# Attention output normalized in feature layout with its product on GpSimd; tanh in place of GELU for the middle chunks; gated-unit weights in 15 parts

## The chip, the core and the metric

The kernel runs on one core of one Trainium2 chip. A core has five engines that run side by side, each with a queue of its own: TensorE (PE; its weight loads are listed as PEld), VectorE (DVE), ScalarE (ACT), GpSimd (POOL) and SyncE (SP), which here only issues transfers (DMA). They wait for one another with semaphores. The metric is device microseconds for one execution, the median of several runs.

## The reference

One transformer block in bfloat16: layer norm, attention with 32 heads of 20 features over 2048 tokens, layer norm, and a gated unit of width 1728 with a GELU in its tanh form.

```python
B, S, D, H, Dh, Df = 1, 2048, 640, 32, 20, 1728

def _A_ref(x, wqkv, wo):
    q, k, v = split of (x @ wqkv) into [3][B, H, S, Dh]
    scores = einsum("bhqd,bhkd->bhqk", q, k) * Dh ** -0.5
    o = einsum("bhqk,bhkd->bhqd", softmax(scores), v)
    return o.reshape(B, S, D) @ wo

def _B_ref(x, w_gate, w_up, w_down):
    return (gelu(x @ w_gate, approximate=True) * (x @ w_up)) @ w_down

h = x + _A_ref(_layernorm(x), wqkv, wo)
return h + _B_ref(_layernorm(h), w_gate, w_up, w_down)
```

## The kernel before, in words

**A planner writes the order.** The kernel does not issue instructions as it goes. Each operation is recorded by `op(...)` with an engine, an estimated duration, a priority, what it reads and writes and which banks of the accumulator memory (PSUM, eight banks of 512 columns) it takes and returns. `Sched.schedule` then plays the program through with these estimates and fixes an order for each engine's queue; `Sched.emit` writes it out with the semaphore waits it needs. Each queue is in order: an instruction that waits holds up all behind it. Where TensorE would be idle too long, the planner puts in filler matmuls (`sc.warm`, which reads `kt_all`). A switch of ScalarE's function table is charged by `MODE_SWITCH`. Nearly all operations recorded through the small helper `I` carry the line of that helper in the profile (L357), so groups are told apart by their tiles.

**Stages.** First come the loads of x, the layer norm and the projections of keys, queries and values (L632). Keys and queries are written to DRAM and read back into `kt_all` and `qt_all` in rows of four heads, 32 partitions each (`k_rows`, `q_rows`; `bounds` is a row that keeps the exponentials in range).

**Attention.** The tokens are cut into seven query chunks, `SIZES = (512, 512, 256, 256, 256, 128, 128)`, called chunks 0 to 6. A chunk is worked off in slots; a slot covers four heads times 512 columns, so there are 8 + 8 + 3 x 4 + 2 x 2 = 32 slots. In a slot TensorE computes scores (L911) into two alternating groups of banks, ScalarE takes their exponentials in bites of 1024 and 1536 columns (`pts`, and `pts2` which lies in `rege`), and TensorE multiplies with the values (L357, `v_all`). For about a ninth of the score tiles VectorE forms the exponential instead: an eviction (L832), then four integer scalings of 128x2048 (`d_exp`). One column of the values is 1, so row 20 of each block of 32 partitions sums the exponentials.

**Epilogue of a slot** (`epilogue`). VectorE copies the output from PSUM to `osb`, with features on partitions and tokens on columns. TensorE transposes it in fp32 (L976), VectorE takes the reciprocal of the sums (L982) and multiplies (L985) into `o_nat`, tokens on partitions.

**After a chunk** (`post`). `o_nat` is transposed back to features (`oT`): for chunk 0 and the last one by TensorE (L577), for the others by a transposing DMA. Then comes the product with `wo`, the residual, the layer norm (its root by a chain of small GpSimd operations, for the last chunk by ScalarE), a transpose to `hnT`, and the gated unit: gate matmuls (L1053) evicted by VectorE (L1088), GELU on ScalarE in place over up to 2048 columns, up matmuls (L1053 again) and their product (L1099), down matmuls (L1110), the sum (L1114) and the store. All this runs as background of the next chunk's attention, at low priority. The last chunk (`tail`) has nothing to run behind; there GELU reads PSUM directly (L1075).

**The gated unit's weights** lie in `regw`, where the projections' data lay before, so they are loaded once all readers of these are through: three big loads and a rest.

```python
load(wg, B_w_gate.rearrange("(a p) f -> p a f", p=128), "wg", 11.0, after=wr)
load(wu, B_w_up.rearrange("(a p) f -> p a f", p=128), "wu", 16.0, after=wr)
load(wd[:, 0:NF - 1, :], B_w_down[0:(NF - 1) * 128, :].rearrange("(a p) d -> p a d", p=128),
     "wd", 21.0, after=wr)
```

Of the kernel before, what the change touches and what calls it, by code (L numbers as in the profile page):

```python
# [7 lines left out]
ALU = mybir.AluOpType  # L8
# [35 lines left out]
class Sched:  # L44
# [46 lines left out]
    def schedule(self):  # L91
# [23 lines left out]
        while done < total:  # L115
# [4 lines left out]
            for e in ENGINES:  # L120
# [208 lines left out]
D_FIRST, D_SPAN = 0, 18  # L329
RSQRT_MAGIC = float(0x5F3759DF)  # L330
# [5 lines left out]
def bass_sequential_preLN__mha_block__glu_gated_geglu__prompt_kernel(  # L336
# [12 lines left out]
    with ExitStack() as es:  # L349
# [10 lines left out]
        def c_mm(n, passes=1):  # L360
            return 0.004 + passes * n / 2400.0
# [31 lines left out]
        o_nat = sb("o_nat", [128, 4, D])  # L393
# [566 lines left out]

        def epilogue(s_, bk):
            s = s_ % 2
            c, gs = slots[s_]
            nq = CHUNKS[c][1]
            nt = nq // 128
            op("dve", I("tensor_copy", osb[:, s, :], PS[:, 512 * 6:512 * 7]), c_dve(512), P_QK,
               reads=[("O", s_)], writes=[("osb", s)], rel=[bk])
            b2 = Bank(*BG[c])
            key = ("bk", sc_id())
            aft = set()  # L970
            tb = base(c)
# [27 lines left out]

        def post(c, banks, tail):  # L1000
# [5 lines left out]
            first = tuple(e_ops) + tuple(last_qk[0]) + tuple(d_ops) if c == 0 else ()  # L1006
            for tt in range(tb, tb + nt):
                t = q0 // 128 + tt - tb
                i = t % 2
                if tail or c == 0:  # L1010
                    transposes(o_nat[:, tt, :], [("on", g, tt) for g in range(NG)], oT[:, :, tt * 128:(tt + 1) * 128],
                               ("hnT", tt), banks, P_EPI, "act" if tail else "dve", after=first)
                else:
                    dma_transposes(o_nat[:, tt, :], [("on", g, tt) for g in range(NG)], oT[:, :, tt * 128:(tt + 1) * 128],
                                   ("hnT", tt), after=first)
# [31 lines left out]
            def mms(k, w, wkey, after):  # L1047
                bk, key = Bank(*banks), ("bk", sc_id())
                for fi in range(min(fn_, NF - k * fn_)):
                    f = k * fn_ + fi  # L1050
                    for a in range(NA):
# [4 lines left out]
                           c_mm(nq), p, mode="full", util=nq / 2400.0, reads=hk + [wkey], writes=[key], acq=[bk] if st else [],  # L1056
# [45 lines left out]
            for tt in range(tb, tb + nt):  # L1102
                t = q0 // 128 + tt - tb
                i = t % 2
                for hf in range(2):
                    bk = Bank(*banks)
                    key = ("bk", sc_id())
                    for f in range(NF):
# [3 lines left out]
                            start=(f == 0), stop=(f == NF - 1)), c_mm(320), p, mode="full", util=0.133, reads=hkeys(f // fn_) + ["wd", "wdz"],  # L1112
# [23 lines left out]
        for s_, (c, gs) in enumerate(slots):  # L1136
            if c == 0:
# [17 lines left out]
                if g == 7:  # L1155
                    wr = tuple(w_readers)
                    load(wg, B_w_gate.rearrange("(a p) f -> p a f", p=128), "wg", 11.0, after=wr)
                    load(wu, B_w_up.rearrange("(a p) f -> p a f", p=128), "wu", 16.0, after=wr)
                    load(wd[:, 0:NF - 1, :], B_w_down[0:(NF - 1) * 128, :].rearrange("(a p) d -> p a d", p=128),
                         "wd", 21.0, after=wr)  # L1160
                    r0 = (NF - 1) * 128 - F0[-1]
                    load(wd[r0:128, NF - 1, :], B_w_down[(NF - 1) * 128:DFF, :], "wd", 2.6, after=wr)
# [40 lines left out]
```

## Time and profile before

| | before |
|---|---|
| median of 3 runs (912.53 to 921.97) | 912.77 us |
| profiled execution, its own time | 915.09 us |
| span in its profile, first to last instruction | 913.2 us |
| TensorE busy | 861.3 us (94%) |
| ScalarE busy | 859.8 us (94%) |
| VectorE busy | 651.7 us (71%) |
| GpSimd busy | 33.2 us (4%) |
| mean granted TensorE clock | 0.993 |
| exponentials on ScalarE (`pts` and `rege` from `ps`) | 825.2 us in 693 instructions |
| function table loads on ScalarE | 16, of 1.28 us each |
| fp32 transposes on TensorE (L976) | 128, 26.8 us |

The groups of a profile are given as: line, engine, operation, out<-in tiles with partitions x elements, count, busy time, mean duration. Busy time of an engine is the union of its instructions' times; TensorE's counts a matmul from start to a modelled end. A row of the timeline has start, duration, engine, line, form and, in brackets, how long the engine was idle before and who ended that.

### The profile page before, as it was taken

To read this page: it belongs to the slowest core of one execution; us is meant where nothing else is said; L and a number is where in the kernel's file an instruction comes from. 1 tells how busy PE (TensorE), PEld (TensorE's weight loads), DVE (VectorE), ACT (ScalarE), POOL (GpSimd) and SP (SyncE) were. 2 spreads that over 40 slices of the span, in tenths; PEclk is the share of its full clock that TensorE was granted. 3 is DMA by queue.
4 is the path that set the end of the run, shared out by engine and by line. 5 is a ranking of instruction groups with operands and counts; after the bars stand their busy time and mean duration, and the time that the engine had idled before them with its cause. 6 is when DMAs were issued, how large, how long until landed. Compare 5 with 4: busy or idle time off the path is not lost.

```text
span 913.2 us, 24238 instructions
## 1 busy us (share of the span) xinstructions
PE 861.3 (94%) x10905; PEld 371.0 (41%) x10905; DVE 651.7 (71%) x1210; ACT 859.8 (94%) x775; POOL 33.2 (4%) x117
## 2 busy tenths in 40 slices
PE   3999999999999999999999998999999999999998
PEld 2532222222232222222344443333444456666677
DVE  7838797888888968877777785665556766654453
ACT  6699999989999989999999999999999999999960
POOL 5000000000001000000000010000001100010100
PEclk9999999999999989999999999999999999999999
DMA  7211020230100380000100101000101001000100
GB/s 259 86 46 32 13 56 6 61 89 22 50 8 12 64 295 1 1 1 1 31 9 17 38 2 31 1 1 2 38 23 45 17 2 24 25 17 10 39 9 23
DMA packets 39519, 34.43 MB, mean 38 GB/s; under 512 B 19436, under 2 KB 36936, under 8 KB 39416
## 3 DMA queue, kind: packets, MB, share of 16 engines
q1 hardware_dynamic: 39416, 32.89, 12.8%
q8 instruction: 85, 1.39, 0.6%
q14 instruction: 18, 0.15, 0.1%
HBM read 20.12 MB, written 8.09 MB: 31 GB/s over the span
## 4 chain that ended last, share of the span: by engine, by line
PE 46%; ACT 45%; DVE 5%; DMA 2%; issue 0%; SPq 0%; DVEq 0%
ACT pts L357 34%; PE ps L911 13%; PE ps L357 11%; ACT rege L357 10%; PE ps L1053 7%; PE ps L632 7%; PE ps L1110 6%; DMA regw<-in_A_wqkv_dram 1%; DVE rege L832 1%; DVE rege L357 1%; DMA rege<-in_A_x_dram 1%; DVE qt_all L832 1%; ACT L357 1%; PE ps L976 1%; DVE qt_all L357 1%; PE ps L577 0%
## 5 line engine op out<-in xcount | busy, mean ns | idle before, releaser
L357 ACT ACTIVATE pts<-ps 128x1536 bf16<-128x1536 f32 x578 | 652.0, 1252 | 14.8 <-PE ps L911 8.8
L911 PE MATMUL ps<-qt_all,kt_all 32*128 32x256 bf16 (+2 forms) x3584 | 322.4, 290 | 20.2 <-ACT pts L357 11.2
L911 PEld LDWEIGHTS ps<-qt_all,kt_all 32*128 32x128 bf16 x3584 | 102.9, 92 | 236.9 <-ACT pts L357 130.2
L832 DVE TENSOR_SCALAR rege<-ps 128x512 int16<-128x512 f32 x200 | 137.4, 688 | 73.3 <-PE ps L911 71.2
L357 ACT ACTIVATE rege<-ps 128x1536 bf16<-128x1536 f32 x115 | 173.2, 1506 | 1.6 <-PE ps L911 1.1
L1053 PE MATMUL ps<-rege,regw 128*128 128x256 bf16 (+2 forms) x980 | 154.5, 290 | 3.8 <-DVE rege L1099 2.3
L357 PE MATMUL ps<-pts,v_all 128*21 128x256 bf16 (+2 forms) x2472 | 135.0, 288 | 0.0
L357 PE MATMUL ps<-rege,v_all 128*21 128x512 bf16 (+2 forms) x1564 | 127.9, 316 | 1.4 <-DVE rege L357 1.0
L832 DVE TENSOR_SCALAR qt_all<-ps 128x512 int16<-128x512 f32 x116 | 79.8, 688 | 49.1 <-PE ps L911 48.4
L1053 PEld LDWEIGHTS ps<-rege,regw 128*128 128x128 bf16 x980 | 74.3, 98 | 57.8 <-issue 26.1
L357 DVE TENSOR_SCALAR rege<-rege 128x2048 int16<-128x2048 int16 x132 | 88.8, 685 | 2.4 <-PE ps L357 1.1
L632 PE MATMUL ps<-regw 128*128 128x512 bf16 (+1 forms) x360 | 87.5, 352 | 2.0 <-DVE rege L832 0.9
L1110 PE MATMUL ps<-regw,rege 128*128 128x320 bf16 x448 | 80.1, 301 | 1.1 <-DVE rege L832 0.5
L357 PEld LDWEIGHTS ps<-pts,v_all 128*21 128x21 bf16 x2472 | 54.3, 91 | 34.6 <-issue 28.3
L357 PEld LDWEIGHTS ps<-rege,v_all 128*21 128x21 bf16 x1564 | 41.3, 91 | 44.0 <-issue 24.4
L357 PE MATMUL ps<-qt_all,v_all 128*21 128x256 bf16 (+2 forms) x1048 | 53.7, 284 | 2.1 <-DVE qt_all L357 2.0
L1099 DVE TENSOR_TENSOR rege<-rege,ps 128x512 bf16<-128x512 bf16 (+1 forms) x53 | 36.0, 680 | 27.2 <-PE ps L1053 27.2
L1110 PEld LDWEIGHTS ps<-regw,rege 128*128 128x128 bf16 x448 | 37.1, 98 | 29.9 <-issue 13.8
L632 PEld LDWEIGHTS ps<-regw 128*128 128x128 bf16 x360 | 29.2, 99 | 47.6 <-issue 26.3
L1088 DVE CAST rege<-ps 128x512 bf16<-128x512 f32 (+1 forms) x53 | 36.1, 680 | 16.2 <-PE ps L1053 16.0
L357 DVE TENSOR_SCALAR qt_all<-rege 128x2048 int16<-128x2048 int16 x70 | 47.0, 686 | 0.7
L357 DVE TENSOR_SCALAR qt_all<-qt_all 128x2048 int16<-128x2048 int16 x69 | 46.3, 685 | 1.7 <-PE ps L357 1.3
(92 smaller groups left out, 483.7 us busy)
## 6 DMA issues: line engine op xcount, KB each, us to landing
rege<-in_A_x_dram SPq DMA_DIRECT2D x6, 640.0 KB, 5.2
q_rows<-regw SPq DMA_DIRECT2D x20, 128.0 KB, 1.7
out_dram<-rege SPq DMA_DIRECT2D x16, 160.0 KB, 1.9
regw<-in_B_w_gate_dram SPq DMA_DIRECT2D x1, 2160.0 KB, 10.6
regw<-in_B_w_up_dram SPq DMA_DIRECT2D x1, 2160.0 KB, 15.6
regw<-in_B_w_down_dram SPq DMA_DIRECT2D x1, 2080.0 KB, 21.6
kt_all<-k_rows SPq DMA_DIRECT2D x12, 160.0 KB
qt_all<-q_rows SPq DMA_DIRECT2D x12, 160.0 KB
```

The lines of the kernel that those rows point to most:

```text
L357: return lambda eng: getattr(eng, method)(*args, **kwargs)
L632: yield op("pe", lambda eng, l=l, r=r, k=k: eng.matmul(bank(bk, n), l, r, start=(k == 0), stop=(k == len(steps) - 1)), c_mm(n), prio, mode ...
L832: d_ops.append(op("dve", lambda eng: eng.tensor_scalar(v[:, 512 * h:512 * h + 512], bank(b), EXP_MUL, -32000.0, ALU.mult, ALU.max), c_dve( ...
L911: return lambda eng: eng.matmul(out()[:, kk * nq:(kk + 1) * nq], kt_all[32 * j:32 * j + 32, g, kt * 128:(kt + 1) * 128], qt_all[32 * j:32 ...
L976: op("pe", lambda eng, tt=tt: eng.transpose(bank(b2)[:, tt * 128:(tt + 1) * 128], osb[:, s, tt * 128:(tt + 1) * 128], identf[:]), c_mm(128 ...
L1053: op("pe", lambda eng, a=a, f=f, fi=fi: eng.matmul(bank(bk)[:, fi * nq:(fi + 1) * nq], w[:, a, F0[f]:F0[f] + 128], hnT[:, a, 128 * tb:128 ...
L1088: cp.append(op("dve", lambda eng, bg=bg, fv=fv, w=w: eng.tensor_copy(fv, bank(bg, w)), c_dve(w), p, reads=[kg], writes=hkeys(k), rel=[bg], ...
L1099: hdone.append(op("dve", lambda eng, bu=bu, fv=fv, w=w: eng.tensor_tensor(fv, fv, bank(bu, w), ALU.mult), c_dve(w), p, reads=[ku] + hkeys( ...
L1110: op("pe", lambda eng, f=f, o=o, hf=hf, bk=bk: eng.matmul(bank(bk, 320), ha_f[:, o:o + 128], wd[:, f, hf * 320:(hf + 1) * 320], start=(f = ...
```

## The change

**Output.** For all chunks but the last, `epilogue` ends after the copy to `osb` and calls the new function `spread`. The four rows of sums go to DRAM and come back as 128 x 16 numbers; VectorE takes their reciprocals there; these go to DRAM and come back as `bsum`, each row repeated over the 32 partitions of its head. GpSimd multiplies `osb` with `bsum` into `on16`, which four transfers store by head into a DRAM tensor of the chunk. `post` then loads `oT` from it in one transfer. `o_nat` remains for the last chunk alone.

**GELU.** For chunks 1 to 5 the eviction of the gate halves it, and the new function `gelu` works on two tiles at a time: with v half the gate, VectorE forms v(a + b v v), ScalarE takes its tanh, VectorE adds 1 and multiplies with v. The buffer `zb` becomes two of 1024, read as float16. The operation's mode is `exp2`, for which the planner charges no table switch. Chunk 0 and the last chunk keep their GELU.

**Weights.** Gate and up weights are loaded in five parts each, the down weights in five, besides the rest; each part waits for the one before the last, and matmuls wait for both of the two semaphores.

```diff
-                if o.mode is not None:
+                if o.mode is not None and o.mode != "exp2":
...
+GELU_A = 2.0 * 0.7978845608028654
+GELU_B = 4.0 * GELU_A * 0.044715
...
-        o_nat = sb("o_nat", [128, 4, D])
+        bsum = sb("bsum", [128, 512], FP32)
+        on16 = sb("on16", [128, 512])
+        o_nat = sb("o_nat", [128, 1, D])
...
-        zb = carve(2 * 512).rearrange("p (i s) -> p i s", i=2)
+        zb = carve(2 * 1024).rearrange("p (i s) -> p i s", i=2)
+        tb16 = zb.bitcast(F16)
...
+        sdr = nc.dram_tensor("sums", [2, 4, 512], FP32, kind="Internal").ap()
+        rdr = nc.dram_tensor("rsums", [2, 4, 512], FP32, kind="Internal").ap()
+        adr = [nc.dram_tensor("attn%d" % c, [NG, 4, DH, n], BF16, kind="Internal").ap() for c, (_, n) in enumerate(CHUNKS[:-1])]
...
+        def spread(s, c, gs, nq):
+            n = len(gs)
+            h = lambda dst, src, reads, key, sem, issue: dma(dst, src, key, reads, sem + str(s), 3.2, P_EPI, issue, keep=False)
+            h(sdr[s], osb[DH:128:32, s, :], [("osb", s)], ("sdr", s), "sa", 0.1)
+            h(rc[:, s, :], sdr[s].rearrange("j (a b) -> (j a) b", b=16), [("sdr", s)], ("rc", s), "sb", 0.4)
+            op("dve", I("reciprocal", rc[:, s, :], rc[:, s, :]), 0.25, P_EPI, reads=[("rc", s)], writes=[("rc", s)])
+            h(rdr[s].rearrange("j (a b) -> (j a) b", b=16), rc[:, s, :], [("rc", s)], ("rdr", s), "sc", 0.4)
+            for j in range(4):
+                h(bsum[32 * j:32 * j + 32, :], rdr[s, j].partition_broadcast(32), [("rdr", s)], ("bs", j), "sd", 0.36)
+            op(POOL, I("tensor_tensor", on16[:], osb[:, s, :], bsum[:], ALU.mult), 1.4, P_EPI,
+               reads=[("osb", s)] + [("bs", j) for j in range(4)], writes=["on16"])
+            for j in range(4):
+                h(adr[c][gs[0]:gs[0] + n, j].rearrange("g e s -> e g s"),
+                  on16[32 * j:32 * j + DH, :].rearrange("p (g s) -> p g s", g=n), ["on16"], ("adr", c, gs[0], j), "se", 0.36)
...
+            if c < len(CHUNKS) - 1:
+                spread(s, c, gs, nq)
+                return
...
+        def gelu(k, w, fv, hk, p):
+            i = gelu_n[0] % 2
+            gelu_n[0] += 1
+            z, zk = tb16[:, i, 0:w], ("zb", i)
+            tt, ts = 0.066 + w * 0.0006, 0.156 + w * 0.00026
+            op("dve", I("tensor_tensor", z, fv, fv, ALU.mult), tt, p, reads=hk, writes=[zk], after=tuple(last_qk[1]))
+            op("dve", I("tensor_scalar", z, z, GELU_B, GELU_A, ALU.mult, ALU.add), ts, p, reads=[zk], writes=[zk])
+            op("dve", I("tensor_tensor", z, z, fv, ALU.mult), tt, p, reads=hk + [zk], writes=[zk])
+            op("act", I("activation", z, z, ACT.Tanh), c_act(w) + 0.04, -1, mode="exp2", reads=[zk], writes=[zk])
+            op("dve", I("tensor_scalar", z, z, 1.0, None, ALU.add), ts, p, reads=[zk], writes=[zk])
+            op("dve", I("tensor_tensor", fv, z, fv, ALU.mult), tt, p, reads=hk + [zk], writes=hk)
...
+            if not tail:
+                op("sp", I("dma_start", oT[:, :, 128 * tb:128 * tb + nq],
+                           adr[c].rearrange("g j e s -> (g j e) s").rearrange("(a p) s -> p a s", p=128)), 0.4, P_EPI,
+                   reads=[("adr", c, gs[0], j) for cc, gs in slots if cc == c for j in range(4)],
+                   writes=[("hnT", tt) for tt in range(tb, tb + nt)], sem=f"oT{c}", lat=2.4 + nq * 0.001, after=first)
...
-                if tail or c == 0:
-                    transposes(o_nat[:, tt, :], ...)
-                else:
-                    dma_transposes(o_nat[:, tt, :], ...)
+                if tail:
+                    transposes(o_nat[:, 0, :], ...)
...
+                    if c:
+                        op("dve", lambda eng, bg=bg, fv=fv, w=w: eng.tensor_scalar(fv, bank(bg, w), 0.5, None, ALU.mult),
+                           c_dve(w), p, reads=[kg], writes=hkeys(k), rel=[bg])
+                        if k % 2 or k == nb - 1:
+                            gelu(k - k % 2, w + 512 * (k % 2), hv(k - k % 2, w + 512 * (k % 2)),
+                                 hkeys(k - 1) * (k % 2) + hkeys(k), p)
+                        continue
...
-                for ks in [list(range(i, min(i + 4, nb))) for i in range(0, nb, 4)]:
+                for ks in [] if c else [list(range(i, min(i + 4, nb))) for i in range(0, nb, 4)]:
...
+                    parts = [(wg[:, a, :], B_w_gate[128 * a:128 * a + 128, :], "wg") for a in range(NA)]
+                    parts += [(wu[:, a, :], B_w_up[128 * a:128 * a + 128, :], "wu") for a in range(NA)]
+                    parts += [(wd[:, f:min(f + 3, NF - 1), :], B_w_down[128 * f:128 * min(f + 3, NF - 1), :].rearrange(
+                        "(a p) d -> p a d", p=128), "wd") for f in range(0, NF - 1, 3)]
+                    ids = []
+                    for i, (dst, src, key) in enumerate(parts):
+                        ids.append(op("sp", I("dma_start", dst, src), 0.35, P_EPI, sem="wp%d" % (i % 2), lat=3.4,
+                                      writes=[(key, i % 2)], after=tuple(wr) if i < 2 else ids[-2:-1]))
```

More of the change, by code (lines that the diff above doesn't have):

```diff
@@ L970, in epilogue @@
             aft = set()
-            tb = base(c)
+            tb = 0
             for g in gs:
@@ L998, in prefetch @@
                after=tuple(e_ops) + tuple(w_readers) if c == 0 else ())
+        gelu_n = [0]
+        def gelu(k, w, fv, hk, p):
[9 more added lines that the diff above has]
+            op("dve", I("tensor_tensor", fv, z, fv, ALU.mult), tt, p, reads=hk + [zk], writes=hk)
         def post(c, banks, tail):
@@ L1009, in post @@
                 i = t % 2
-                if tail or c == 0:
-                    transposes(o_nat[:, tt, :], [("on", g, tt) for g in range(NG)], oT[:, :, tt * 128:(tt + 1) * 128],
-                               ("hnT", tt), banks, P_EPI, "act" if tail else "dve", after=first)
-                else:
-                    dma_transposes(o_nat[:, tt, :], [("on", g, tt) for g in range(NG)], oT[:, :, tt * 128:(tt + 1) * 128],
-                                   ("hnT", tt), after=first)
+                if tail:
+                    transposes(o_nat[:, 0, :], [("on", g, 0) for g in range(NG)], oT[:, :, tt * 128:(tt + 1) * 128],
+                               ("hnT", tt), banks, P_EPI, "act", after=first)
                 for hf in range(2):
@@ L1055, in mms @@
                             start=(a == 0), stop=(a == NA - 1)),
-                           c_mm(nq), p, mode="full", util=nq / 2400.0, reads=hk + [wkey], writes=[key], acq=[bk] if st else [],
+                           c_mm(nq), p, mode="full", util=nq / 2400.0, reads=hk + [(wkey, 0), (wkey, 1)], writes=[key], acq=[bk] if st else [],
                            after=after if st else ())
@@ L1111, in post @@
                             bank(bk, 320), ha_f[:, o:o + 128], wd[:, f, hf * 320:(hf + 1) * 320],
-                            start=(f == 0), stop=(f == NF - 1)), c_mm(320), p, mode="full", util=0.133, reads=hkeys(f // fn_) + ["wd", "wdz"],
+                            start=(f == 0), stop=(f == NF - 1)), c_mm(320), p, mode="full", util=0.133, reads=hkeys(f // fn_) + [("wd", 0), ("wd", 1), "wd2", "wdz"],
                            writes=[key], acq=[bk] if f == 0 else [], after=hdone[-2:] if f == 0 else ())
```

6 lines of the change are left out of this document (1 added, 5 removed).

## The prediction

> **What bounds the kernel now.** I read the busy times first, then busy time by stage, then the ScalarE timeline, then what lies behind the last exponential. These are the page's totals, and busy time in five windows (columns: from and to, length, then busy us and instruction count of PE, PEld, DVE, ACT, POOL; granted clock; DMA share; GB/s).
>
> ```profile
> PE 861.3 (94%) x10905; PEld 371.0 (41%) x10905; DVE 651.7 (71%) x1210; ACT 859.8 (94%) x775; POOL 33.2 (4%) x117
> ```
>
> ```profile
> 47.00:265.00 218.00, 206.80 (x1722) 61.54 (x1719) 174.65 (x310) 211.80 (x188) 0.00 (x0) 0.99 0.14 39
> 265.00:480.00 215.00, 206.06 (x1935) 64.94 (x1934) 171.30 (x294) 211.94 (x185) 3.31 (x15) 0.98 0.16 44
> 480.00:740.00 260.00, 250.46 (x3643) 112.03 (x3641) 177.99 (x321) 259.36 (x226) 10.58 (x42) 1.00 0.08 19
> 740.00:873.20 133.20, 129.57 (x2969) 85.96 (x2967) 72.77 (x136) 132.83 (x115) 7.17 (x28) 1.00 0.08 20
> 873.20:913.20 40.00, 36.16 (x420) 29.41 (x417) 17.26 (x39) 11.07 (x15) 0.00 (x0) 1.00 0.05 18
> ```
>
> From 47 to 873.2 us ScalarE is idle for 10.3 of 826 us (6.2, 3.1, 0.6 and 0.4), so each microsecond that leaves ScalarE there moves the last exponential forward. TensorE looks as full, but what it does besides scores and values fills gaps: from 480 us on ScalarE is idle for 1.0 of 393 us, whatever it waits for. VectorE has 20% to 45% left by stage. Behind the last exponential (873.24) come 40.0 us in which ScalarE works 11 and TensorE 36. So the time is ScalarE's stream plus a tail.
>
> This is what stands between the exponentials of chunk 4 (ScalarE timeline: start, us, form):
>
> ```profile
> 866.33 1.28 ACT L357 ACT_TABLE_LOAD   x1
> 867.62 3.28 ACT L357 ACTIVATE rege<-rege 128x2048 bf16<-128x2048 bf16 x2
> 870.92 1.28 ACT L357 ACT_TABLE_LOAD   x1
> 872.22 1.02 ACT L357 ACTIVATE pts<-ps 128x1024 bf16<-128x1024 f32 x1
> ```
>
> Two table loads enclose the GELU of each chunk: 5.89 us from 866.33 to 872.22. Chunks 2 and 3 cost the same, chunk 1 (7168 columns) 9.07 us.
>
> **GELU as tanh.** Removed from ScalarE's full stretch: 9.07 + 3 x 5.89 = 26.7 us (chunk 0 keeps its GELU). Added: the built order shows 16 tanhs of 1024 columns and 3 of 512 before the last exponential, and no table load beside them (6 loads in all, 16 before). An exponential of 1024 follows the one before by 0.92 us, a pass over 1024 columns in SBUF lasts 1.04 alone; I take 0.95. For 512, 0.60 alone less the 0.1 of overlap: 0.5. 16 x 0.95 + 3 x 0.5 = 16.7. **Gain 10.0 us**, between 8.3 (all at 1.04, and 0.6) and 10.6 (0.92, 0.48).
>
> VectorE pays. Each pair of gate tiles gets three products and two scalings over 1024 columns. Rows: a bf16 product of 1024 takes 690 ns, of 512 413; a scaling of 2048 takes 685, of 512 286, hence about 419 for 1024. So 2.91 us for each of 17 pairs, 1.81 for each of three single tiles, 2.4 for the last 768: 57 us. Leaving VectorE: 30 of 32 reciprocals (254 ns, 7.6), the products at L985 of all but chunk 6 (17.2) and four copies at L586 (1.9); a reciprocal in SBUF comes back 30 times, at 0.17 to 0.25 (6). Net +36: 688 us, 75% of the span. If the mixed float16 and bfloat16 products ran at the pace of an fp32 eviction (512 in 0.68, so about 1.2 for 1024), 27 us more, 78%. Between 250 and 320 us VectorE is 90% busy while ScalarE idles 0.1 us, so I cost both at nothing. The cover is VectorE's idle time; without it a tanh waits for its input, with all exponentials queued behind it. The halving at the gate's eviction replaces a copy of the same size (688 against 685 ns): nothing. **Bounds 0 and +5** (19 tanhs, each 0.26 late).
>
> **Normalization.** TensorE loses 120 fp32 transposes of 128 columns (26.8 us for 128 of them: 25.1) and 20 bf16 ones (2.2). TensorE ended almost no ScalarE wait after chunk 1, so in the stream this is worth nothing; it moves background work forward. The built order has the following behind the last score matmul: 260 matmuls of 128 columns instead of 274, none of 256 instead of 70, 86 of 320 instead of 112. At 57, 115 and 142 ns (127 in 7.25 us, 27 in 3.12, 28 in 3.98) that is 0.8 + 8.1 + 3.7 = 12.6 us less.
>
> Of this the tail gets little. From 873.24 to the feature transposes at 888.17, the chain of chunk 6 (values, copy, reciprocal, output product, statistics, square root) waits for TensorE for 1.4 + 0.7 + 0.7 and for a late chunk-5 GELU with two table loads, 1.9 (884.1 to 886.0): 4.7 saved. But VectorE now runs chunk 5's scaling chain between these steps (two products of 0.6, one of 0.5, two scalings of 0.3, a longer eviction: 2.7 less 0.8 that lay there before), and the second tanh holds ScalarE's copy of the transposes by about 0.8: 2.7 back. What follows the transposes is 210 matmuls of 128 and 56 of 320 in both. **Tail -2.0 us**, between +2 and -5.
>
> SyncE gets 11 small transfers for each of 30 slots, 330 at 0.31 to 0.55 us of issue, some 116 us of an idle queue, and loses 11 transposing ones (1.2 each). The chain is: sums out, sums in, reciprocal, back out, four broadcasts, product, four stores, and one load per chunk. Six landings in a row at 1.6 (bounds) to 2.7 us (transposes), 3 of issue, 1.5 of arithmetic: 14 to 21 us where transposes and copies took about 4. It is covered by the next chunk's slots of 25 us (two for the last such chunk). Without the cover chunk 5 comes up to 17 us later into the tail, which then pays perhaps 5. Small transfers also queue behind big ones:
>
> ```profile
> 186.70 0.41 SPq L357 DMA_DIRECT2D rege<-in_A_x_dram  x1
> 187.16 0.55 SPq L357 DMA_DIRECT2D qt_all<-bounds  x1
> ...
> 192.12 1.02 ACT L357 ACTIVATE pts<-ps 128x1024 bf16<-128x1024 f32 x1 [3.40 <-PE ps L911]
> ```
>
> The bounds go behind 640 KB, and ScalarE waits 3.40 us. The order keeps this pair, so this stays. The new reciprocal waits in VectorE's queue for such a transfer: what is late behind it are the evictions of scores, then value matmuls.
>
> **Weights in 15 parts.** 6.4 MB, two parts of some 430 KB in flight instead of all at once; the three loads landed 22 us after issue. At the 400 GB/s of that stretch the data alone take 16, with 2 us of landing behind each pair 31; I take 24, and 0 for the time: the gate's first matmul comes about two slots after the first part. At worst +2.
>
> **GpSimd's product.** No product of this size is in the trace. Below: a memset of 128x512 fp32, 0.54 us. Above: a one-input select over 160 columns is 0.35, 0.95 ns a column beyond 0.2, so two inputs over 512 give 1.2; with one VectorE operation waited for, 1.9. It is nearest to the select; I take 1.2. What it does to VectorE is the larger matter:
>
> ```profile
> 546.05 0.20 POOL L357 TENSOR_TENSOR rs<-rs,nw 128x4 f32<-128x4 f32 x1
> 546.33 0.70 POOL L357 TENSOR_TENSOR nw<-rs 128x4 f32<-128x4 f32 x1
> ...
> 546.27 0.69 DVE L357 TENSOR_SCALAR qt_all<-rege 128x2048 int16<-128x2048 int16 x1
> ```
>
> The same small product takes 0.20 alone and 0.70 when a 2048-column scaling started 0.06 earlier: it ends 0.07 behind that. So the two exclude each other, and a product of 1.2 us that starts first should hold the next such scaling for up to 1.2. Thirty of these cost VectorE up to 36 us. What reaches ScalarE is less: TensorE waits for about 90 of 318 such scalings already (27 us in all), and scores have room, since their weight loads wait for ScalarE 360 times, 0.36 us each. One product in three, 0.35 us each: **+3.5 us**, bounds 0 and 30 x 1.0.
>
> The Trainium skill's "SBUF — State Buffer", section "Who interferes with whom", says that GpSimd and such a VectorE operation hold a shared pair of ports for the whole instruction and the second one fully blocks. The rows agree for GpSimd as the second; no run here shows VectorE as the second. By this rule the 3.5 us stand; if VectorE were not held as the second, the sum below would be -12.0 and the time 900.8.
>
> **Sum.** -10.0 - 2.0 + 3.5 = -8.5. The profiled execution's span of 913.2 becomes 904.7, its own time 915.09 becomes 906.6. That execution lies 2.3 above the median of the runs (912.77); on the median: **904.3 us**. 1% is 9.1 us, about what a measurement of this kernel can tell from no change.
>
> **Rivals.** *Lock:* GpSimd's product holds VectorE at a scaling that value matmuls wait for, every slot; TensorE's queue is in order, so scores come late too. For it: the rows above, and 27 us of such waits now. Against it: idle VectorE time and 130 us in which TensorE waits for ScalarE. It eats 12.0 us from 0.40 us a slot on; at 0.8 the time is 912.8 + 12 = 925.
>
> *Clock:* with the transposes gone TensorE has less to do while the weights arrive. From 318 to 334 us the granted clock was 0.70 and ScalarE lost 2.6 of 16 us. The built order ends the projections two slots earlier and starts the gate at the same slot: up to 50 us thin, with 27 filler matmuls there instead of 7. At half of it, 25 x 2.6/16 = 4, at all of it 8: the gain is gone, about 911.
>
> *Clean:* no new stall, and half of the ScalarE idle time of the first two stages (9.3) leaves with the transposes: -10 - 2 - 4.6, 896.
>
> That the change doesn't do what it says is out for the tables: the built order has 6 loads.
>
> **How the numbers follow.** Forecast 0.58 (900 to 909 by its own bounds, a little under half of it under 903.6); clean 0.15; clock 0.13; lock 0.14, nearly all over 922. Faster by over 1%: 0.27 + 0.15 = 0.42; slower by over 1%: 0.13; within: 0.45. The range leaves out the upper part of the lock and the lower end of clean: 895 to 919.
>
> **What would show it.** Right: 6 table loads; last exponential at 864 to 869 us; tanhs with no idle time before them; 37 to 40 us behind the last exponential; TensorE busy near 835. The lock: GpSimd's products over 1.2 us, VectorE's 2048-column scalings over 0.69, ScalarE idle in stages beyond 480 us. The clock: granted clock under 0.9 over more than 16 us. I am wrong if VectorE passes 80%, or if ScalarE waits for tanh inputs.

## The result, and the profile after

The changed kernel takes 919.41 us (median of 20 executions, 914.35 to 924.12) against 913.02 (20 executions, 911.88 to 921.97): ratio 1.0053, interval 1.0031 to 1.0074, so 3 to 7 us slower. The forecast was 904.3, the range ended at 919.0. The profiled execution is one of the shortest: 914.51 us, span 912.7. The twenty differ by TensorE's mean granted clock: seven with 0.983 to 0.985 take 914.35 to 917.40, thirteen with 0.970 to 0.978 take 918.19 to 924.12.

The page's totals after the change:

```profile
PE 851.5 (93%) x10792; PEld 358.4 (39%) x10792; DVE 688.1 (75%) x1263; ACT 849.0 (93%) x775; POOL 75.2 (8%) x147
```

VectorE is where the prediction put it (688). ScalarE lost 10.8 us. TensorE lost only 9.8, though 120 fp32 and 20 bf16 transposes went (27): it also ran slower, and the planner put in 54 filler matmuls instead of 27. Busy time by window, cut at the new last exponential (871.84; before 873.24):

```profile
47.00:265.00 218.00, 206.23 (x1700) 58.23 (x1697) 174.99 (x303) 213.65 (x189) 12.04 (x9) 0.98 0.22 58
265.00:480.00 215.00, 200.64 (x1851) 62.69 (x1852) 165.47 (x274) 205.62 (x178) 15.71 (x22) 0.98 0.21 57
480.00:740.00 260.00, 249.00 (x3650) 110.50 (x3650) 200.89 (x361) 258.09 (x231) 22.52 (x52) 0.99 0.13 33
740.00:871.84 131.84, 130.21 (x2993) 83.15 (x2994) 90.68 (x170) 130.89 (x117) 12.79 (x32) 1.00 0.14 30
871.84:912.70 40.86, 33.01 (x392) 26.79 (x389) 18.33 (x44) 8.32 (x14) 0.00 (x0) 0.95 0.05 17
```

From 47 us to the last exponential ScalarE has 7.7 us less to do (808.3 instead of 815.9) and idles 6.3 more (16.6 instead of 10.3). The second window alone has 6.3 more: 9.4 of 215 us, 3.1 before. The first has 1.9 less, the third and fourth together 1.9 more. The last exponential comes 1.4 earlier instead of 6.5, and the tail is 40.9 instead of 38. Most of the new idle time has one place (timeline, several engines):

```profile
268.96 0.38 SPq L359 DMA_DIRECT2D rege<-attn  x1
274.82 1.49 PE L640 MATMUL ps<-wo,rege 128*128 128x320 bf16 x5 [4.78 <-DMA rege<-attn]
276.90 1.45 ACT L359 ACTIVATE pts<-ps 128x1536 bf16<-128x1536 f32 x1 [5.37 <-PE ps L919]
```

The load of `oT` for chunk 0 (`rege<-attn`) lands 5.8 us after issue, where the planner reckoned 2.9. Five matmuls with `wo` wait for it at the head of TensorE's queue, with the next scores behind them; ScalarE waits 5.4 us for these. Then TensorE comes back at half clock (windows of 5 us):

```profile
270.00:275.00 5.00, 0.22 (x5) 0.14 (x2) 0.93 (x2) 1.53 (x2) 0.00 (x0) 0.56 0.99 314
275.00:280.00 5.00, 5.00 (x33) 1.14 (x31) 2.63 (x5) 2.06 (x2) 0.00 (x0) 0.50 0.39 107
```

The DMA share of 0.99 comes with weight parts under way. ScalarE works 63.05 of the 70 us from 250 to 320 (69.87 before).

The tanhs do what was said: one follows an exponential and is followed by the next after 0.95 us, and no table load stands between 392.70 (behind chunk 0's GELU) and 871.86 (ScalarE timeline).

```profile
840.63 1.07 ACT L359 ACTIVATE qt_all<-qt_all 128x1024 f16<-128x1024 f16 x1
841.58 3.29 ACT L359 ACTIVATE pts<-ps 128x1024 bf16<-128x1024 f32 x3
...
871.86 1.28 ACT L359 ACT_TABLE_LOAD   x1
```

### The profile page after: what moved, and what is told of

Same layout as the page of the kernel before. It is cut to its first block, busy times and chain, and to the rows that moved or that the text cites. A ratio compares the mean times of both kernels' runs of the same rounds, so it can differ in the third digit from the quotient of the medians.

```text
span 912.7 us, 24454 instructions
## 1 busy us (share of the span) xinstructions
PE 851.5 (93%) x10792; PEld 358.4 (39%) x10792; DVE 688.1 (75%) x1263; ACT 849.0 (93%) x775; POOL 75.2 (8%) x147
## 4 chain that ended last, share of the span: by engine, by line
PE 47%; ACT 44%; DVE 6%; DMA 2%; issue 1%; SPq 0%; DVEq 0%
ACT pts L359 34%; PE ps L919 14%; PE ps L359 11%; ACT rege L359 9%; PE ps L1095 8%; PE ps L640 7%; PE ps L1159 6%; DVE rege L840 1%; ACT qt_all L359 1%; DVE rege L359 1%; DVE qt_all L359 1%; DVE stats L359 1%; DMA attn<-on 1%; DMA rege<-attn 1%; PE ps L585 1%
## 5 line engine op out<-in xcount | busy, mean ns | idle before, releaser
L359 ACT ACTIVATE pts<-ps 128x1536 bf16<-128x1536 f32 x578 | 654.0, 1254 | 20.5 <-PE ps L919 14.0
L1095 PE MATMUL ps<-rege,regw 128*128 128x256 bf16 (+2 forms) x980 | 160.8, 293 | 4.5 <-ACT rege L591 2.2
L359 PE MATMUL ps<-rege,v_all 128*21 128x512 bf16 (+2 forms) x1564 | 130.1, 316 | 1.9 <-DVE rege L359 1.9
L359 POOL TENSOR_TENSOR on<-osb,bsum 128x512 bf16<-128x512 f32 x30 | 41.4, 1379 | 668.8 <-DMA bsum<-rsums 668.8
L359 DVE TENSOR_SCALAR rege<-rege 128x2048 int16<-128x2048 int16 x132 | 91.4, 709 | 2.6 <-PE ps L359 2.0
L1159 PE MATMUL ps<-regw,rege 128*128 128x320 bf16 x448 | 82.2, 302 | 1.1 <-DVE rege L1120 0.5
L359 DVE TENSOR_SCALAR qt_all<-qt_all 128x2048 int16<-128x2048 int16 (+3 forms) x111 | 63.5, 584 | 2.6 <-PE ps L359 1.0
```

Of the source, the lines that this page charges most:

```text
L359: return lambda eng: getattr(eng, method)(*args, **kwargs)
L1095: op("pe", lambda eng, a=a, f=f, fi=fi: eng.matmul(bank(bk)[:, fi * nq:(fi + 1) * nq], w[:, a, F0[f]:F0[f] + 128], hnT[:, a, 128 * tb:128 ...
L1159: op("pe", lambda eng, f=f, o=o, hf=hf, bk=bk: eng.matmul(bank(bk, 320), ha_f[:, o:o + 128], wd[:, f, hf * 320:(hf + 1) * 320], start=(f = ...
```

## The experiments

The theory at first was that chunk 0's output chain crosses the weights and stalls TensorE, and that tanh brings its 10 us. The runs with one part each broke half of it. Every ratio is to the kernel before, run beside the kernel in question.

**One part at a time.** Each is the kernel before with one part of the change: `gelu()` with the larger `zb` (first), `spread()` with the load of `oT` (second), the 15 `parts` (third).

> The kernel before with one part of the change alone: tanh in place of GELU for chunks 1 to 5. Output path and weight loads are those of before. Theory 1 (the tanh brings what the prediction said, and the loss sits in chunk 0's output chain): 10 us less than before, 901 to 905 us, 6 table loads, last exponential 9 to 11 us earlier. Rival (VectorE's 36 us more delay evictions or tanh inputs, or TensorE's clock falls with the other order): 908 to 914 us, with ScalarE idle over 4 us more than before in the stages from 320 us on.

> The kernel before with the other part alone: output normalized in feature layout with the product on GpSimd; GELU and the three big weight loads are those of before. Theory 1 (chunk 0's output stores and its load of oT lie behind the weight loads; the product with wo stands ahead of scores in TensorE's queue and holds them, and the clock falls): 6 to 14 us more than before, 919 to 927, with the wait at the product with wo over 5 us, since three loads at once leave less room than parts. Rival (GpSimd's product holds VectorE in every slot): also more, but spread over all stages, ScalarE idle 0.2 to 0.4 us a slot from 320 us on. Second rival (it was the weight parts): within 2 us of before, and the wait at wo under 2 us.

> The kernel before with the weight loads in 15 parts alone. Theory 1: no output chain crosses the weights there, so within 1.5 us of before, 911 to 915. Rival (the parts by themselves come too late for the gate and thin TensorE's work): 3 to 8 us more, granted clock under 0.8 between 300 and 340 us.

Measured: tanh alone 916.92 us, ratio 1.0044 (1.0028 to 1.0059), with 8 table loads instead of the 6 expected; output path alone 932.43, 1.0230 (1.0197 to 1.0262); parts alone 914.10, 1.0005 (0.9994 to 1.0016). So tanh by itself loses 4 us, outside both the theory's range and the rival's, and the rival's new idle time of ScalarE isn't there. Up to the last exponential and behind it, tanh alone:

```profile
47.00:859.60 812.60, 780.23 (x10108) 312.68 (x10106) 621.60 (x1119) 802.41 (x707) 19.20 (x76) 0.99 0.12 31
859.60:916.50 56.90, 50.26 (x567) 41.10 (x564) 37.57 (x82) 14.97 (x20) 1.75 (x10) 1.00 0.07 21
```

ScalarE idles as little as before (10.2 us), and the last exponential comes 13.6 us earlier, more than forecast, with six tanhs behind it where the changed kernel has two. The stretch behind it grew from 40.0 to 56.9: more of the gated units of chunks 4 and 5 came out behind the attention. TensorE's total is 862.9 us, before 861.3, and it idles 6.6 us of the stretch behind, before 3.8.

The output path alone is worse than its theory had it (919 to 927), and far worse than with the parts. SyncE's queue and TensorE's longest wait there:

```profile
264.87 12.27 SPq L357 DMA_DIRECT2D sums<-osb  x1
277.18 0.44 SPq L357 DMA_DIRECT2D rege<-attn  x1
```

```profile
PE ps L637 <- DMA rege<-attn: 17.4, 1, 17.4
```

Behind the three big weight loads (issued at 262.7 to 264.3) the next small transfer takes 12.27 us to issue, and the load of `oT` stands behind it in SyncE's queue. The 15 parts cut this wait from 17.4 to 4.8 us; alone they are worth nothing.

**Which engine sets the end.** After tanh alone had moved time from the stream to the tail, two kernels took work from one engine only. In the kernel before:

```diff
-                for ks in [list(range(i, min(i + 4, nb))) for i in range(0, nb, 4)]:   # GELU
+                for ks in [] if c else [list(range(i, min(i + 4, nb))) for i in range(0, nb, 4)]:
```
```diff
-                    for f in range(NF):                                                # down product
+                    for f in range(NF) if tail or c == 0 else range(0, NF, 2):
...
```

> The kernel before with the GELU of chunks 1 to 5 left out, so that the product takes the gate as it is: 26.7 us of passes and table loads leave ScalarE's stream, and nothing is added anywhere. ScalarE theory (the prediction's: time is ScalarE's stream plus a tail that stays): 22 to 27 us less than before, 886 to 891 us. Rival (TensorE is as full; its gated-unit work that filled the stream comes out behind it): last exponential 22 to 27 us earlier, but the stretch behind it 10 to 20 us longer, 898 to 908 us, with TensorE busy over 95% of the span.

> The kernel before in which the down product of chunks 1 to 5 leaves out every second of its 14 steps: 154 matmuls of 320 columns fewer, at 142 ns 21.9 us of TensorE; ScalarE and VectorE keep all their work. TensorE theory (its whole work sets the end, wherever ScalarE's stream ends): 12 to 20 us less than before, 893 to 901 us, last exponential within 3 us of 873, the stretch behind it 12 to 20 us shorter. ScalarE theory (the prediction's): only what lies behind the last exponential counts, some 14 to 40 of these matmuls, 2 to 5 us less: 908 to 911.

Measured: without the GELU 912.30, ratio 0.9989 (0.9980 to 0.9998); with half of the down product 903.78, 0.9902 (0.9884 to 0.9919). Windows up to the last exponential and behind it, without GELU and with half of the down product:

```profile
47.00:844.20 797.20, 752.32 (x9943) 303.23 (x10002) 581.47 (x1031) 788.13 (x691) 15.00 (x71) 0.99 0.12 31
844.20:909.80 65.60, 61.38 (x663) 50.64 (x660) 30.94 (x64) 6.78 (x12) 2.56 (x14) 1.00 0.10 26
```

```profile
47.00:874.00 827.00, 774.88 (x10234) 325.13 (x10292) 602.95 (x1070) 819.46 (x713) 18.58 (x85) 1.00 0.12 31
874.00:901.10 27.10, 20.02 (x248) 15.29 (x245) 10.10 (x27) 6.69 (x12) 0.00 (x0) 0.99 0.04 13
```

Take 26.7 us from ScalarE, and the last exponential comes 29.0 earlier, the tail grows by 25.6, and 1 us is won. Take 154 matmuls, by the forecast's estimate 21.9 us, from TensorE, and the last exponential stays, the tail falls from 40.0 to 27.1, and 9 us are won. In the kernel before TensorE's total work sets the end; ScalarE's full stream lies beside it. The sizes were missed: the forecast for the half product (12 to 20) was too high, as ScalarE's stream still ends at 874 and 27 us come behind it; without the GELU the rival had 898 to 908 and TensorE over 95% busy (93% in the profile, which has 64 matmuls fewer than weight loads, so some records are missing). The direction is clear in both.

**The two places of loss.** The changed kernel once more, then with the load of `oT` planned later, and with the weights behind that load.

```diff
-                   ..., sem=f"oT{c}", lat=2.4 + nq * 0.001, after=first)
+                   ..., sem=f"oT{c}", lat=2.4 + nq * 0.001 if c else 9.0, after=first)
```
```diff
-                    wr = tuple(w_readers)              # at slot 7, ahead of post(0)
+                wr = tuple(w_readers) + (ot0,)         # in post(0), ot0 its load of oT; parts as they were
```

> The changed kernel once more, for a profile of another of its executions: they lie between 914 and 924 us, and the one profiled first is among the shortest. Clock theory (what lies between 914 and 919 to 924 is TensorE at half clock at a thin place of the first slots): if this execution is over 917 us, its profile shows a stretch of 10 to 25 us at a granted clock near 0.50 between 70 and 140 us, and ScalarE idle there by as much as it is longer. Rival (it is GpSimd's product or late transfers): no such stretch, waits of 1 to 2 us spread over the slots.

> The changed kernel with one planner number changed: the load of oT for chunk 0 is taken to land after 9.0 us instead of 2.9, so that the product with wo stands about one slot quarter later in TensorE's queue, behind more scores. Theory 1: the wait of 4.8 us at wo and the low clock at 270 to 285 us vanish, 5 to 7 us less than the changed kernel, 912 to 914, and ScalarE's busy time between 250 and 320 us is over 68 of 70 us. Rival (what the typical executions lose is low clock elsewhere, at other thin places): less than 2 us gained.

> The changed kernel with the 15 weight parts issued behind chunk 0's load of oT instead of ahead of its output stores. Queue theory (stores and load of chunk 0 lie behind weight parts in the DMA engines): the last stores and the load of oT land in 2 to 3.5 us each instead of 5.9 and 5.7, the wait at wo falls from 4.8 to under 1.5 us, ScalarE works 67 us or more of 250 to 320 instead of 63, and the time is 3 to 6 us less than the changed kernel, 913 to 916. Rival (the chain of six transfers is as long without the weights): wait at wo over 3 us and the time within 2 us of the changed kernel's. The gate starts later; if that thins TensorE, the clock falls between 290 and 330 us.

The second profile of the changed kernel is of an execution of 917.78 us. Its windows from 70 us on:

```profile
70.00:75.00 5.00, 4.04 (x24) 0.97 (x23) 4.90 (x12) 5.00 (x5) 0.00 (x0) 0.79 0.32 95
75.00:80.00 5.00, 5.00 (x31) 1.04 (x30) 3.01 (x6) 3.43 (x4) 0.00 (x0) 0.50 0.04 11
80.00:85.00 5.00, 4.82 (x29) 0.79 (x25) 1.70 (x3) 3.17 (x4) 0.00 (x0) 0.50 0.27 72
85.00:90.00 5.00, 4.62 (x21) 1.26 (x21) 3.38 (x7) 3.13 (x4) 1.27 (x1) 0.50 0.06 16
90.00:95.00 5.00, 5.00 (x49) 1.53 (x45) 4.37 (x8) 4.40 (x5) 0.00 (x0) 1.00 0.00 0
```

From about 73 to 90 us TensorE ran at half clock and looks busier for it; ScalarE lost some 5 us. The execution profiled first has a clock of 1.00 there. Planned late: 915.34, ratio 1.0015 (0.9995 to 1.0036). Weights behind the load: 915.60, 1.0022 (1.0000 to 1.0045); there the wait at `wo` was 1.0 us, and ScalarE worked 65.9 of the 70 us from 250 to 320, not the 67 expected. Planned late it worked 68.0 and nothing waited at `wo`, but the 912 to 914 expected were missed; that profile has half clock elsewhere, a mean of 0.61 from 70 to 105 us. By medians both win about 4 us on the changed kernel; the intervals just touch its own, so the size is uncertain to 2 us either way. Neither got rid of the longer executions: their clocks still go down to 0.972 and 0.974.

**What kept the clock up.** In the kernel before, four fp32 transposes stand between the scores at 73.4 to 75 us. These kernels keep transposes and throw the result away, for all eight slots of chunk 0, for the first slot, or for the first and third:

```diff
             if c < len(CHUNKS) - 1:
                 spread(s, c, gs, nq)
+                if c == 0:          # or s_ < 1, or s_ in (0, 2)
+                    b2, key = Bank(*BG[c]), ("bk", sc_id())
+                    for qt in range(4):  # eng.transpose(bank(b2)[:, 128 * qt: ...], osb[:, s, ...], identf)
+                        ...
                 return
```

> The changed kernel in which the eight slots of chunk 0 keep the four fp32 transposes of before on TensorE, at the same place in the plan; their result is thrown away. TensorE gets 32 transposes more, 7 us. Clock theory (these transposes filled the thin places of the first slots; without them the clock falls to half): 3 to 6 us less than the changed kernel, 913 to 916, granted clock between 70 and 140 us at 0.97 or more; the wait at the product with wo stays. Rival (TensorE has no room, and the clock falls for another reason): 0 to 5 us more, 919 to 924.

> The changed kernel in which one slot, the first, keeps its four fp32 transposes on TensorE (result thrown away): four matmuls, 0.9 us, at 73 to 75 us; of the rest of TensorE's order only a few neighbouring groups change places, and the product with wo stays where it was. Clock theory: the stretch at half clock from 75 to 90 us shrinks to the 3 to 5 us that it has in the kernel before, most executions come at a mean clock of 0.983 or more, median 914 to 916.5, 3 to 5 us less than the changed kernel (919.4), with the wait of some 4.8 us at wo unchanged. Rival (what keeping 32 transposes brought was the later place of wo alone): 918 to 920.

> The same with the first and the third slot: eight matmuls, 1.8 us, the second four at 122 us, where the profile of the changed kernel shows the second stretch at half clock (120 to 130 us, 2.7 us of ScalarE lost). Clock theory: 2 to 3 us less than with the first slot alone, median 912 to 914, granted clock 0.95 or more from 105 to 140 us. Rival: as with the first slot alone.

Measured: all eight slots 911.47, ratio 0.9986 (0.9963 to 1.0009); first slot 915.04, 1.0012 (0.9999 to 1.0026); first and third 915.67, 1.0011 (0.9995 to 1.0028). Four matmuls more, 0.9 us of work, made the kernel about 4 us faster (the interval does not overlap that of the changed kernel, 1.0031 to 1.0074), with the wait at `wo` unchanged (4.5 us). Its twelve executions lie between 913.82 and 917.07, none of them among the long ones of the changed kernel. The window from 70 to 105 us in the execution of 917.78, with the first slot's transposes, and before:

```profile
70.00:105.00 35.00, 33.10 (x222) 8.36 (x222) 24.50 (x44) 29.12 (x25) 1.27 (x1) 0.76 0.12 33
```

```profile
70.00:105.00 35.00, 32.96 (x251) 9.33 (x251) 27.99 (x49) 31.85 (x28) 1.27 (x1) 0.90 0.13 36
```

```profile
70.00:105.00 35.00, 32.80 (x267) 9.74 (x271) 28.78 (x54) 33.84 (x31) 0.00 (x0) 0.95 0.06 18
```

The other profiles bear on it too. From 70 to 83 us the granted clock is 0.61 to 0.69 in four of the seven profiles that have the new output path without the first slot's transposes, and 1.00 in the other three. With these transposes it is 0.87 in six of seven and 1.00 in one. So they cut the first low stretch short. They don't keep the clock up behind it: from 83 to 105 us it is 0.69 in four of these seven.

The third slot's transposes brought nothing: the low clock of 120 to 130 us moved to 130 to 135. That expectation failed. Keeping all eight also put `wo` behind more scores, and no load is waited for there, against what was expected; so its 6 us by the ratios (8 by medians) hold both repairs. It isn't a full cure: its profiled execution, the longest of its twelve, still fell to 0.50 at 90 us (0.76 from 70 to 105, where 0.97 was expected), and took 921.36; two more take 916.77 and 919.50.

The Trainium skill's "TensorE: Matmul & The Clock Gate", "Part 4: PE-mode transpose", says that a TensorE transpose doesn't count as busy "the same way" for the clock gate. The run with four of them added speaks against it for these fp32 transposes: the clock from 70 to 83 us is 0.87 with them and 0.61 in the execution of 917.78 us, the rest of TensorE's order nearly unchanged. A few neighbouring groups did change places, so it isn't shown that the transposes alone did this.

**Tanh and GpSimd where TensorE is relieved.** Both keep the eight slots' transposes; one has the GELU of before, the other the product on VectorE (`op(POOL, ...on16...)` becomes `op("dve", ...)`).

> The changed kernel with the transposes of chunk 0 kept (as in the run before) and with the GELU of before in place of tanh; the new output path and the 15 weight parts stay. If tanh brings its 10 us where TensorE has been relieved of transposes: 5 to 9 us more than with tanh (911.5), 916 to 920. If TensorE still sets the end and tanh's chain of VectorE steps holds up the last chunks: within 2 us of it or less, 906 to 913.

> The changed kernel with the transposes of chunk 0 kept and the product of output and reciprocal on VectorE instead of GpSimd: 30 products of 128x512 fp32, about 0.7 us each, 21 us more on VectorE, and none on GpSimd. Lock theory (GpSimd's products hold VectorE and through it ScalarE): 3 to 6 us less than with GpSimd (911.5), 905 to 908, VectorE's 2048-column scalings back at 685 ns. Rival (the lock costs little): 910 to 915.

Measured: with GELU 918.82, ratio 1.0052 (1.0032 to 1.0072), against 0.9986 with tanh: here tanh is worth 6 us. So more than half of the 10 us is there where TensorE has the transposes of chunks 1 to 5 less to do. With the product on VectorE 921.01, 1.0073 (1.0045 to 1.0101): 8 us worse, not better, outside both theory and rival. VectorE's scalings are back at 681 to 687 ns, as the lock theory had it. The order differs elsewhere, and the clock was low (0.88 from 110 to 180 us), so the time doesn't price the lock; it only shows no gain in avoiding it.

The lock itself is in the changed kernel's profile, GpSimd's products and two groups of VectorE's scalings (685 and 686 ns before):

```profile
L359 POOL TENSOR_TENSOR on<-osb,bsum 128x512 bf16<-128x512 f32 x30 | 41.4, 1379 | 668.8 <-DMA bsum<-rsums 668.8
```

```profile
L359 DVE TENSOR_SCALAR rege<-rege 128x2048 int16<-128x2048 int16 x132 | 91.4, 709 | 2.6 <-PE ps L359 2.0
L359 DVE TENSOR_SCALAR qt_all<-rege 128x2048 int16<-128x2048 int16 x70 | 48.5, 703 | 1.7 <-PE ps L359 1.3
```

```profile
462.45 1.33 POOL L359 TENSOR_TENSOR on<-osb,bsum 128x512 bf16<-128x512 f32 x1 [22.11 <-DMA bsum<-rsums]
462.61 0.49 DVE L1163 TENSOR_TENSOR rege<-ps,rege 128x320 bf16<-128x320 f32 x1
463.02 1.31 DVE L359 TENSOR_SCALAR qt_all<-qt_all 128x2048 int16<-128x2048 int16 x1
```

A scaling that starts inside a product waits it out: 1.31 us instead of 0.69. By the Trainium skill ("SBUF — State Buffer", "Who interferes with whom") whichever of the two issues second is fully blocked; the trace now has VectorE as the second, and it agrees. But few scalings start so: over the four groups of 318 it is 6.4 us, 0.2 a product.

**Fillers.** The planner's thresholds raised, with kept transposes, alone, with the late plan, in the kernel before, and with both repairs:

```diff
-WARM_WIN, WARM_MIN = 3.4, 0.5
-PAD_WIN, PAD_MIN = 3.4, 0.42
+WARM_WIN, WARM_MIN = 3.4, 0.6
+PAD_WIN, PAD_MIN = 3.4, 0.5
```

> The changed kernel with the transposes of chunk 0 kept, and the planner's two thresholds for filler matmuls raised from 0.5 to 0.6 and from 0.42 to 0.5 of the last 3.4 us: 67 fillers instead of 58, and more padding at value matmuls. Clock theory: fewer executions with a stretch at half clock, median 907 to 910 at a mean clock of 0.994 or more. Rival (TensorE has no time to give): 913 to 917.

> The changed kernel with only the planner's two filler thresholds raised, from 0.5 to 0.6 and from 0.42 to 0.5; no transposes are kept. Clock theory: 2 to 5 us less than the changed kernel, 914 to 917, because the wait at the product with wo stays, with granted clock over 0.95 between 70 and 140 us. Rival (only the kept transposes, or the order they bring, help): 918 to 921.

> The changed kernel with the filler thresholds raised and the load of oT for chunk 0 planned at 9.0 us: both repairs, nothing kept of the old output path. Theory (wait at wo and low clock are the whole loss, 4 us each): 907 to 911 us, mean clock 0.990 or more, no wait over 1.5 us at wo. Rival: 912 or more, if the fillers cost TensorE what they save.

> The kernel before with the same raised filler thresholds: a control. Theory (before loses 1 to 2 us to low clock, so fillers have little to repair and cost TensorE time): within 2 us of before, 912 to 916. Rival (fillers help any order of this kernel, and the gain seen with them says nothing on the change): 907 to 909.

> The changed kernel with the transposes of chunk 0 kept, the filler thresholds raised, and the load of oT planned at 9.0 us. Theory (with the transposes kept the product with wo already stood behind enough scores): within 2 us of the version without the late plan (907.9), 906 to 910. Rival (a part of the wait at wo was left there): 903 to 905.

| kernel | median us | ratio to before |
|---|---|---|
| kept transposes, fillers | 907.89 | 0.9940 (0.9919 to 0.9960) |
| fillers | 916.47 | 1.0021 (0.9998 to 1.0043) |
| fillers, late plan | 912.51 | 0.9990 (0.9963 to 1.0018) |
| before, fillers | 928.05 | 1.0159 (1.0140 to 1.0179) |
| kept transposes, fillers, late plan | 910.18 | 0.9978 (0.9961 to 0.9995) |

The first beats both kernels: by the ratios 5.5 us under before and 10 under the changed one. Its own profile, the longest of its nine executions, still has a granted clock of 0.76 from 70 to 105 us, and so have the two with fillers but no transposes, where over 0.95 was expected. Fillers alone win 3 us on the changed kernel by the ratios, with overlapping intervals; the wait at `wo` is 3.2 us there, and how they win is open. With the late plan it is 6 us, and the median is the rival's (912 or more). The control failed as a control: the order moved a transposing transfer of chunk 0 behind the weights, and its issue took 13.55 us (SyncE's queue, then the matmul that waited):

```profile
304.78 0.53 SPq L357 DMA_DIRECT2D regw<-in_B_w_down_dram  x1
305.35 13.55 SPq L357 DMA_TRANSPOSE rege<-xn_t  x1
```

```profile
324.44 1.89 PE L1053 MATMUL ps<-rege,regw 128*128 128x512 bf16 x4 [8.62 <-DMA rege<-xn_t]
```

It says nothing on what fillers cost, but is the same stall at another place. The last row should have been within 2 us of the first; by the ratios it is 3.5 us longer. In neither profile does `wo` wait for its load, so with the transposes kept there was nothing left to repair there.

## Why the prediction was wrong, point by point

The miss of 15.1 us splits as: last exponential 871.84 instead of 866.7, 5.1; tail 40.9 instead of 38.0, 2.9; median 4.9 above the profiled execution, where the prediction took it 2.3 below as before, 7.2.

- **"The time is ScalarE's stream plus a tail."** This step failed first. The two terms aren't independent: what leaves the stream comes back in the tail (GELU left out: 29.0 out, 25.6 back). The prediction saw TensorE 94% busy and argued that its other work "fills gaps"; that work has to be done somewhere. Take it from TensorE instead (half of the down product), and 9 us are won with the last exponential in its place.
- **Tanh, -10.0.** The counts and prices held (19 tanhs, 0.95 us each, no wait for a tanh). VectorE at 688 is luck: tanh alone adds 45.5 us to it where 57 were reckoned, and the output path alone takes off 10.0 where the terms give 20.7 (the products at L985 take 17.2 us with chunk 6, 15.8 without, and the lock adds 6.4). ScalarE's work in the stream fell by 7.7 instead of 10; the exponentials became 2 to 3 ns longer (1.7 us over 693). Alone tanh costs 4 us, with TensorE relieved it wins 6.
- **Transposes "worth nothing in the stream".** Wrong in sign: without them the first slots lost some 5 us at half clock in the execution of 917.78 us, and thirteen of the twenty have as low a mean clock. The rival called clock had the mechanism and nearly the size (4 to 8), but another place: from 320 to 390 us, where the weights arrived before, the clock is now 1.00 (0.95); they now arrive from 262 us on, and there it fell behind the wait at `wo`.
- **SyncE's chain "covered by the next chunk's slots of 25 us".** Not for chunk 0. Its load of `oT` was planned at 2.9 us and landed at 5.8, and what waited was not late background but the head of TensorE's queue. The prediction let `oT` delay chunk 5 and priced the weights apart, each at nothing; it didn't ask what the six landings cost while the weights are on their way.
- **The x load, "so this stays".** The pair stayed, but the wait went: the bounds are now issued at 178.3 us behind the x load at 177.4, some 9 us sooner than before, and ScalarE works 70.00 of 180 to 250 us (66.49), as it does with the output path alone. That gain of 3.5 hid part of the loss.
- **Weights in parts, 0.** Right alone (1.0005), and with the new output path they save most of a 17 us wait.
- **GpSimd, +3.5.** From 390 to 860 us ScalarE idles 4.0 us, before 1.2: 2.8, near the forecast, but not shown to be the lock's. With the product on VectorE, where the scalings are back at 681 to 687 ns, it still idles 3.7 there (in another order); with the output path alone 3.6, with tanh alone 1.3. So the new idle time comes with the output path, and no run shows it to be the lock. The rival called lock is out.
- **Tail, -2.0.** It is +0.9. The feature transposes come 1.5 us sooner behind the last exponential (13.5 us, before 15.1), not 2.8 as the terms up to there give: the root no longer waits for a late GELU, but the statistics now stand between halvings and scalings of chunk 5 on VectorE, and ScalarE waits 6.1 us for them. The copy behind the transposes, held by tanhs, costs 0.8 as forecast. The term left out lies behind it, in matmuls that are the same "in both": their stretch takes 24.7 us, before 23.0. TensorE, which before had down products of chunk 5 to do there, now stands idle, and then runs at half clock. This is the stretch from 10 to 20 us behind the last exponential, before and after:

```profile
883.24:893.24 10.00, 10.00 (x111) 8.10 (x110) 4.51 (x13) 5.16 (x6) 0.00 (x0) 1.00 0.09 33
```

```profile
881.84:891.84 10.00, 6.00 (x53) 4.69 (x51) 6.56 (x19) 3.96 (x6) 0.00 (x0) 0.83 0.00 0
```

What stays open: why a low stretch lasts 3 us in one execution and 27 in another, how the 6 to 8 us of keeping all transposes divide beyond the 4 of the first slot, and what idles ScalarE beyond 390 us.

## What to carry to other kernels

When two engines are both over 90% busy, ask of each microsecond taken from one where the other's work goes; leaving out a suspected cost entirely (here the GELU) prices the best case in one run. Work removed from a matmul engine in a thin stretch can cost more than it took, so cost a removal by what it does to the granted clock there. A small transfer that a queue's head waits for must be timed against the big loads issued around it, not alone.

## What was not expected of the hardware

- A transfer of a few KB behind three loads of about 2.1 MB took 12.27 us to issue on SyncE, a transposing one 13.55, where others take 0.3 to 0.6 and 1.2.
- Half clock, once granted in the first slots, lasted 3.4 us (0.87 over the 13 us from 70 to 83, first slot kept) to 27 us (0.61 over the 35 us from 70 to 105, planned late) with TensorE busy 95% of these 35 us. In the clock records of the traces the low stretches last 3.4, 6.8, 10.2, 13.7, 17.1, 20.5 or 27.3 us, but for some that end with the program. The mean clock differed between executions of one kernel: 914.35 us at 0.985, 924.08 at 0.970.
